# A decode kernel that streams 282 MB: re-dealing 224 weight rows over the DMA engines, turning q by one transpose, and re-dealing the softmax copies

## The chip, the cores and the metric

The kernel runs on one core of one Trainium2 chip. The metric is the device time of one execution in microseconds (us). "Before" and "changed" are the two kernels. Each ratio comes from rounds on one chip. Runs of different sessions, which the text also sets side by side, ran on three chips or more; the medians of the kernel before in the three sessions of experiments agree within 0.06 us.

## The reference

```python
xn = layernorm(x)                        # x: 4 x 1 x 640
# A: attention with a cache, B=4, H=32, Sk=4096, Dh=128
q = (xn @ wq) split in 32 heads
o = softmax(q @ k_cache.T * Dh**-0.5) @ v_cache
A = o @ wo
# B: gMLP, Fh = 864
z = gelu(xn @ w_in); z1, z2 = z[:864], layernorm(z[864:])
B = (z1 * (w_sp * z2 + b_sp)) @ w_out    # w_out: 864 x 640
out = x + A + B
```

The k and v caches are 268 of the 282 MB that are read. Each element of them is used once.

## The kernel before

Five slots of 32 KiB per partition hold everything large. The weights of the head (wq, w_in, w_out) lie in slots that later hold k and v. The caches come in units of 8 MiB (one batch row, eight heads), each issued as soon as its slots are free; all large loads go through the SyncE queue.

```python
wq = at_slot(0, n_q)...                                  # 5 MB
nc.sync.dma_start(out=wq, in_=...)
nc.scalar.dma_start(out=x_bf, in_=x_flat)
nc.sync.dma_start(out=w_in, in_=...)                     # 2.2 MB
nf = (FC - 1) * P                                        # FC = 7: six blocks of 128 rows, one of 96
nc.sync.dma_start(out=w_out[:, 0:FC - 1, :], in_=B_w_out[0:nf, :]...)
nc.sync.dma_start(out=w_out[:FL, FC - 1, :], in_=B_w_out[nf:Fh, :])
nc.sync.dma_start(out=sb_bf[:, 0:1], in_=B_w_sp)
nc.sync.dma_start(out=sb_bf[:, 1:2], in_=B_b_sp[None, :])
... # layernorm of x, masks
load_unit(seq[0])                                        # first k unit
for r in range(HP):                                      # q, copied four times for the matmul turn
    op = nc.vector.tensor_copy if r < 2 else nc.scalar.copy
    for a in range(2):
        op(out=q4[:, :, 2 * a:2 * a + 2, r, :], in_=q4_in[:, :, a])
for h in range(HG):
    for kw in range(4):
        nc.tensor.matmul(q3_ps[:, kw, h, :], lhsT=q4[:, h, kw]..., rhs=SelJ..., start=True, stop=True)
... # gMLP branch
def softmax(g):                                          # once per group of heads, four times in all
    ... # maximum, exp, transpose of p into pT
    for hp in range(HP):
        for q in range(4):
            op = nc.vector.tensor_copy if q < 2 or (hp == 0 and q == 2) else nc.scalar.copy
            op(out=xd[...], in_=pT[...])
    z_fill(g, 0)                                         # masks xd into Zb, the weights of the V matmuls
    z_fill(g, 1)
```

Of the kernel before, what the change touches and what calls it, by code (L numbers as in the profile page):

```python
# [16 lines left out]
def kernel(  # L17
# [20 lines left out]
    P = 128  # L38
# [17 lines left out]
    Fh = F2 // 2  # L56
    FC = (Fh + P - 1) // P
    FL = Fh - (FC - 1) * P
    NOUT = A_wo.shape[1]
# [5 lines left out]
    const = ctx.enter_context(tc.tile_pool(name="const", bufs=1))  # L65
    small = ctx.enter_context(tc.tile_pool(name="small", bufs=2))
    ktpool = ctx.enter_context(tc.tile_pool(name="ktpool", bufs=2))
    ppool = ctx.enter_context(tc.tile_pool(name="ppool", bufs=3))
# [8 lines left out]
    def misc_ps(shape, dtype):  # L77
        misc_ctr[0] += 1
        return ps_m.tile(shape, dtype, tag="misc", name=f"misc{misc_ctr[0]}")
# [5 lines left out]
    def at_slot(i, n, off=0):  # L85
        return kv[:, i * SL + off:i * SL + off + n]
# [6 lines left out]
    n_q = DC * H * Dh  # L93
    wq = at_slot(0, n_q).rearrange("p (c n) -> p c n", c=DC)
    nc.sync.dma_start(out=wq, in_=A_wq.rearrange("(p c) n -> p c n", c=DC))

    ln_t = at_slot(0, 8 * D, n_q)
    x_bf = ln_t[:B, 0:D]
    nc.scalar.dma_start(out=x_bf, in_=x_flat)

    x_res = const.tile([32, NO2], BF16)
    nc.vector.memset(x_res[:], 0.0)

    n_in = DC * F2
    w_in = at_slot(2, n_in).rearrange("p (c f) -> p c f", c=DC)
    nc.sync.dma_start(out=w_in, in_=B_w_in.rearrange("(p c) f -> p c f", c=DC))
    w_out = at_slot(2, FC * NOUT, n_in).rearrange("p (c n) -> p c n", c=FC)

    nf = (FC - 1) * P
    nc.sync.dma_start(out=w_out[:, 0:FC - 1, :], in_=B_w_out[0:nf, :].rearrange("(p c) n -> p c n", p=P))  # L110
    nc.sync.dma_start(out=w_out[:FL, FC - 1, :], in_=B_w_out[nf:Fh, :])  # L111
    sb_bf = const.tile([1, 2], BF16)
    nc.sync.dma_start(out=sb_bf[:, 0:1], in_=B_w_sp)
    nc.sync.dma_start(out=sb_bf[:, 1:2], in_=B_b_sp[None, :])

# [51 lines left out]
    ones_f = const.tile([P, P], F32)  # L167
    nc.vector.memset(ones_f[:], 1.0)
    eps_t = const.tile([P, 1], F32)
    nc.vector.memset(eps_t[:], eps)  # L170

# [27 lines left out]
    QZ = const.tile([P, B, 4, NE, QL], BF16)  # L199
    nc.vector.memset(QZ[:].rearrange("p b a e l -> p (b a e l)").bitcast(F32), 0.0)  # L200

# [8 lines left out]
    SelPe = const.tile([P, NE, HP, NE, B], F32)  # L210
    nc.vector.memset(SelPe[:].rearrange("p x h e b -> p (x h e b)"), 0.0)
    for e in range(NE):
# [6 lines left out]
    SelR = const.tile([P, B, HG, B], F32)  # L219
    nc.vector.memset(SelR[:].rearrange("p x h b -> p (x h b)"), 0.0)  # L220
    for b in range(B):
# [17 lines left out]
    for i in range(2):  # L239
        zt = const.tile([P, NW, HG, 4], BF16, name=f"Zb{i}")  # L240
        nc.vector.memset(zt[:].rearrange("p a h c -> p (a h c)").bitcast(F32), 0.0)
        Zb.append(zt)
# [13 lines left out]

    q4 = at_slot(0, HG * Dh * HP, n_q + 8 * D).rearrange("p (h k r j) -> p h k r j", h=HG, k=4, r=HP)
    q4_in = q4_ps[:].rearrange("p (h a j w) -> p h a w j", h=HG, a=2, w=2)
    for r in range(HP):
        op = nc.vector.tensor_copy if r < 2 else nc.scalar.copy  # L260
        for a in range(2):
            op(out=q4[:, :, 2 * a:2 * a + 2, r, :], in_=q4_in[:, :, a])  # L262

    SelJ = const.tile([P, NG, B], BF16)
    nc.vector.tensor_copy(out=SelJ[:], in_=ident_bf[:].rearrange("p (j r) -> p j r", j=NG)[:, :, 0:B])
    q3_ps = misc_ps([P, 4, HG, NG * B], F32)
    for h in range(HG):
        for kw in range(4):
            nc.tensor.matmul(q3_ps[:, kw, h, :], lhsT=q4[:, h, kw].rearrange("p r j -> p (r j)"),
                             rhs=SelJ[:].rearrange("p j b -> p (j b)"), start=True, stop=True)  # L270
    q3 = const.tile([P, 4, HG, NG * B], BF16)
    nc.vector.tensor_copy(out=q3[:], in_=q3_ps[:])


    zT_ps = misc_ps([P, 2, FC, B], F32)
    for part in range(2):
        for fc in range(FC):
            n = P if fc < FC - 1 else FL
            f0 = part * Fh
            for c in range(DC):  # L280
                if fc < FC - 1:
                    w = w_in[:, c, f0:f0 + nf].rearrange("p (f a) -> p a f", a=FC - 1)[:, fc, :]
                else:
                    w = w_in[:, c, f0 + nf:f0 + Fh]
                nc.tensor.matmul(zT_ps[:n, part, fc, :], lhsT=w,
                                 rhs=xnT[:, c, 0:B], start=(c == 0), stop=(c == DC - 1))
    zT = const.tile([P, 2, FC, B], F32)
    nc.vector.memset(zT[:], 0.0)
    uT = const.tile([P, FC, 32], BF16)
    nc.vector.memset(uT[:], 0.0)  # L290
    nc.scalar.activation(out=zT[:, :, 0:FC - 1, :], in_=zT_ps[:, :, 0:FC - 1, :], func=ACT.Gelu_apprx_tanh)
    nc.scalar.activation(out=zT[:FL, :, FC - 1, :], in_=zT_ps[:FL, :, FC - 1, :], func=ACT.Gelu_apprx_tanh)

    one_bf = const.tile([1, P], BF16)
    nc.vector.memset(one_bf[:], 1.0)
    sb_ps = misc_ps([P, 2], F32)
# [37 lines left out]
    for fc in range(FC):  # L334
        n = P if fc < FC - 1 else FL
        nb = B if fc > 1 else 32
        r0 = 64 * (fc % 2)
        for hf in range(NH):
            nc.tensor.matmul(proj[r0 + 32 * hf:r0 + 32 * hf + nb, 0:NO2], lhsT=uT[:n, fc, 0:nb],
                             rhs=w_out[:n, fc, hf * NO2:(hf + 1) * NO2], start=(fc < 2), stop=False)  # L340


    def fill_qz(g):
        for hp in range(HP):
            r0 = 32 * hp
            nc.gpsimd.tensor_copy(out=QZ[r0:r0 + 32, :, :, :, 8 + 8 * hp],  # L346
                                  in_=q3[r0:r0 + 32, :, NE * hp:NE * hp + NE, g * B:g * B + B].rearrange("p a e b -> p b a e"))

# [3 lines left out]
    def emit_K(u, k):  # L352

        g, b = divmod(u, B)
        hh = first.get(u, 0) ^ (k // 4)
        qp, kh = k // 2 % 2, k % 2
        t0 = 2 * TC * (2 * hh + qp)
        kw = unit(("k", u), t0, t0 + 2 * TC).bitcast(F32).rearrange("p (t w) -> p t w", w=KW)[:, :, 32 * kh:32 * kh + 32]
        kT = ktpool.tile([P, 2 * TC * 32], F32, tag="kT", name="kT")
        nc.vector.transpose(kT[:].rearrange("p (t r) -> p t r", r=32), kw)  # L360
        if ("S", g) not in state:
            S_new = ps_s.tile([P, NE, TC, M], F32, tag="S", name="S")
            state[("S", g)] = S_new
        S_ps = state[("S", g)]
        kb = kT[:].bitcast(BF16).rearrange("p (i t e m w) -> p i t e m w", i=2, e=NE, m=M, w=2)
        w0 = 8 - (b * C2 + hh)
        for w in range(2):
            for e in range(NE):
                for i in range(2):
                    q = 2 * qp + i  # L370
                    nc.tensor.matmul(S_ps[32 * q:32 * q + 32, e], lhsT=QZ[:, b, 2 * kh + w, e, w0:w0 + 32],  # L371
                                     rhs=kb[:, i, :, e, :, w], start=(b == 0 and k < 4 and kh == 0 and w == 0),
                                     stop=(b == B - 1 and k >= 4 and kh == 1 and w == 1))
# [21 lines left out]
    def z_fill(g, b):  # L395
        xd = state[("xd", g)]
        for hp in range(HP):
            r0 = 32 * hp
            src = xd[r0:r0 + 32, C2 * b:C2 * b + C2].rearrange("p x q (y c) -> p (x q y) c", c=4)
            for e in range(NE):  # L400
                dst = Zb[b % 2][r0:r0 + 32, :, NE * hp + e, :]
                mk = MkE[r0:r0 + 32, e:e + 1]
                if b == 0 and e == 0:
                    nc.vector.tensor_scalar(out=dst, in0=src, scalar1=mk, scalar2=None, op0=ALU.mult)
                else:
                    nc.scalar.activation(out=dst, in_=src, func=ACT.Copy, scale=mk)  # L406

    def softmax(g):
# [13 lines left out]
        for hp in range(HP):  # L422
            for q in range(4):
                op = nc.vector.tensor_copy if q < 2 or (hp == 0 and q == 2) else nc.scalar.copy
                op(out=xd[32 * hp:32 * hp + 32, :, q, :], in_=pT[32 * q:32 * q + 32, :, hp, :].rearrange("p t x -> p x t"))  # L425
# [101 lines left out]

    o_1 = const.tile([64, NO2], F32)
    nc.vector.tensor_copy(out=o_1[:], in_=proj[0:64, 0:NO2])
# [9 lines left out]

    o_bf = const.tile([64, NO2], BF16)  # L540
    nc.vector.tensor_tensor(out=o_bf[:], in0=last[:], in1=o_1[:], op=ALU.add)
# [30 lines left out]
```

## Time and profile before

| | before |
|---|---|
| median (lowest to highest), 3 runs | 665.26 us (665.23 to 665.98) |
| read from HBM | 282.25 MB, 425 GB/s over the span |
| DMA share, 2 to 650 us | 1.00 |
| DMA share, 655 to 660 us | 0.40 |
| VectorE, TensorE, ScalarE busy | 54%, 45%, 12% |

The way to read it is to ask first which resource has no idle time. Here it is the 16 DMA engines: their share is 1.00 from 2 to 650 us. They only have idle time at the end (0.40 from 655 to 660 us), when some of them are finished and others are not. The lines are in the prediction below.

### The profile page before, as it was taken

What the parts mean: (1) busy time and instruction counts of PE and PEld (TensorE: products, weight loads), DVE (VectorE), ACT (ScalarE), POOL (GpSimd) and SP (SyncE); (2) the same over time, 40 slices, a digit from 0 to 9 for tenths busy, and PEclk for the clock granted to TensorE, in tenths of its full rate; (3) what the DMA queues carried; (4) which work ended last, traced back from release to release, by engine and by line L of the source; (5) the groups of instructions that cost most, each with busy time, mean ns of one, the idle gap of its engine ahead of it and who ended that gap; (6) DMA issues with size and microseconds to landing.
All of it is one profiled execution on the core that took longest, in us unless ns stands there. A gap on an engine that the chain in (4) does not pass through costs nothing.

```text
span 663.5 us, 5584 instructions
## 1 busy us (share of the span) xinstructions
PE 298.7 (45%) x2366; PEld 111.7 (17%) x2366; DVE 359.9 (54%) x341; ACT 82.6 (12%) x169; POOL 6.2 (1%) x24
## 2 busy tenths in 40 slices
PE   0525765266073457235436075433607244624146
PEld 0401211022021122111112022111202112211012
DVE  5338999656190849509156286745628084940002
ACT  0300000440100000530200000070100000053200
POOL 0000000000000000000000000000000000000000
PEclk9758779678577786667758577865857778756777
DMA  9999999999999999999999999999999999999996
GB/s 368 457 439 420 409 441 440 439 436 436 423 431 440 419 426 448 435 432 423 436 439 432 431 423 438 437 440 435 416 435 436 443 435 412 444 423 436 426 419 248
DMA packets 6949, 282.61 MB, mean 426 GB/s; under 512 B 792, under 2 KB 1164, under 8 KB 1548
## 3 DMA queue, kind: packets, MB, share of 16 engines
q1 hardware_dynamic: 6908, 282.25, 98.8%
q8 instruction: 18, 0.29, 0.2%
q14 instruction: 7, 0.06, 0.0%
q10 hardware_dynamic: 16, 0.01, 0.0%
HBM read 282.25 MB, written 0.01 MB: 425 GB/s over the span
## 4 chain that ended last, share of the span: by engine, by line
DMA 73%; DVE 12%; issue 11%; PE 2%; ACT 1%; SPq 0%; DVEq 0%; ACTq 0%
DMA kv<-in_A_k_cache_dram 65%; DVE kT L360 11%; DMA kv<-in_A_v_cache_dram 4%; DMA kv<-in_A_wo_dram 3%; PE O L442 2%; DVE xd L425 0%; PE last L537 0%; ACT Zb L406 0%; ACT p L414 0%; DVE pT L418 0%; DVE m L378 0%; PE misc L383 0%; PE S L371 0%; SPq L111 0%; ACT xd L425 0%
## 5 line engine op out<-in xcount | busy, mean ns | idle before, releaser
L360 DVE STREAM_TRANSPOSE kT<-kv 128x2048 f32<-128x2048 f32 x128 | 282.8, 2275 | 126.1 <-DMA kv<-in_A_k_cache_dram 126.1
L371 PE MATMUL S<-kT,QZ 128*32 128x512 bf16 x1024 | 192.8, 511 | 230.4 <-DVE kT L360 230.4
L371 PEld LDWEIGHTS <-QZ 128*32 128x32 bf16 x1024 | 61.4, 112 | 355.6 <-issue 336.7
L442 PE MATMUL O<-kv,Zb 128*32 128x512 bf16 x1024 | 76.3, 464 | 59.7 <-ACT Zb L406 30.2
L449 DVE TENSOR_SCALAR R<-O,Mk 128x128 f32<-128x128 f32 x16 | 5.6, 351 | 129.8 <-PE O L442 129.8
L406 ACT ACTIVATE Zb<-xd,MkE 32x256 bf16<-32x256 bf16 x112 | 51.4, 498 | 106.0 <-PE O L442 104.6
L414 ACT ACTIVATE p<-S,negmax 128x512 bf16<-128x512 f32 x8 | 5.4, 683 | 400.4 <-DVE negmax L392 400.4
L442 PEld LDWEIGHTS <-Zb 128*32 128x32 bf16 x1024 | 33.1, 114 | 102.4 <-issue 58.3
L459 PE MATMUL misc<-R,SelR 128*32 128x128 f32 x32 | 6.4, 281 | 26.0 <-DVE R L451 26.0
L425 ACT COPY xd<-pT 32x256 bf16<-32x256 bf16 x28 | 17.2, 613 | 5.7 <-DVE pT L418 5.2
L451 DVE SCALAR_TENSOR_TENSOR R<-O,Mk,R 128x128 f32<-128x128 f32 x48 | 16.8, 351 | 1.7
L425 DVE COPY xd<-pT 32x256 bf16<-32x256 bf16 x36 | 13.1, 364 | 0.6
L346 POOL COPY QZ<-q 32x32 bf16<-32x32 bf16 x16 | 5.1, 321 | 421.6 <-PE S L371 394.8
L418 DVE STREAM_TRANSPOSE pT<-p 128x1024 bf16<-128x1024 bf16 x4 | 5.0, 1245 | 6.3 <-ACT p L414 6.3
L459 PEld LDWEIGHTS misc<-R,SelR 128*32 128x32 f32 x32 | 2.2, 107 | 33.5 <-DVE R L451 24.8
L262 DVE CAST kv<-q 128x512 bf16<-128x512 f32 x4 | 2.5, 684 | 9.4 <-PE q L254 9.4
L378 DVE TENSOR_REDUCE m<-S 128x2 f32<-128x1024 f32 x4 | 4.9, 1225 | 4.9 <-PE S L371 4.9
L383 PE MATMUL misc<-dg,ones_f 128*128 128x256 f32 x8 | 3.7, 558 | 7.6 <-DVE dg L380 7.6
L254 PE MATMUL q<-kv,xnT 128*32 128x512 bf16 x40 | 4.2, 600 | 5.3 <-DMA kv<-in_A_wq_dram 5.3
L462 DVE SCALAR_TENSOR_TENSOR om<-misc,rinv,MkH 32x1024 bf16<-32x1024 f32 x4 | 5.1, 1271 | 2.0 <-PE misc L459 2.0
L430 PE MATMUL misc<-rowsum,SelPe 128*32 128x1 f32 x16 | 2.1, 203 | 9.0 <-ACT p L414 9.0
L191 PE MATMUL misc<-ident_bf,kv 4*128 4x4 bf16 x5 | 0.4, 178 | 10.7 <-DVE kv L187 10.7
(97 smaller groups left out, 70.1 us busy)
## 6 DMA issues: line engine op xcount, KB each, us to landing
kv<-in_A_k_cache_dram SPq DMA_DIRECT2D x8, 4096.0 KB, 29.8
kv<-in_A_v_cache_dram SPq DMA_DIRECT2D x1, 6144.0 KB
kv<-in_A_wq_dram SPq DMA_DIRECT2D x1, 5120.0 KB, 15.6
kv<-in_A_wo_dram SPq DMA_DIRECT2D x3, 1280.0 KB, 20.9
kv<-in_B_w_in_dram SPq DMA_DIRECT2D x1, 2160.0 KB
kv<-in_A_v_cache_dram SPq DMA_DIRECT2D x1, 2048.0 KB
kv<-in_B_w_out_dram SPq DMA_DIRECT2D x1, 960.0 KB
kv<-in_A_wo_dram SPq DMA_DIRECT2D x1, 640.0 KB, 22.4
```

The lines of the kernel that those rows point to most:

```text
L346: nc.gpsimd.tensor_copy(out=QZ[r0:r0 + 32, :, :, :, 8 + 8 * hp], in_=q3[r0:r0 + 32, :, NE * hp:NE * hp + NE, g * B:g * B + B].rearrange("p ...
L360: nc.vector.transpose(kT[:].rearrange("p (t r) -> p t r", r=32), kw)
L371: nc.tensor.matmul(S_ps[32 * q:32 * q + 32, e], lhsT=QZ[:, b, 2 * kh + w, e, w0:w0 + 32], rhs=kb[:, i, :, e, :, w], start=(b == 0 and k < ...
L406: nc.scalar.activation(out=dst, in_=src, func=ACT.Copy, scale=mk)
L414: nc.scalar.activation(out=p_bf[:, :, e, :], in_=S_ps[:, e], func=ACT.Exp, bias=negmax[:, e:e + 1], scale=scale, accum_out=rowsum[:, e:e + 1])
L418: nc.vector.transpose(pT[:].rearrange("p t h x -> p (t h x)"), p_bf[:].rearrange("p t e m -> p (t e m)"))
L425: op(out=xd[32 * hp:32 * hp + 32, :, q, :], in_=pT[32 * q:32 * q + 32, :, hp, :].rearrange("p t x -> p x t"))
L442: nc.tensor.matmul(O_ps[32 * q:32 * q + 32, :, :], lhsT=Zb[b % 2][:, w].rearrange("p h c -> p (h c)"), rhs=vv[:, w * 4 * Dh:(w + 1) * 4 * ...
L449: nc.vector.tensor_scalar(out=R, in0=O_ps[:, 0, :], scalar1=Mk4[:, 0:1], scalar2=None, op0=ALU.mult)
L451: nc.vector.scalar_tensor_tensor(out=R, in0=O_ps[:, c, :], scalar=Mk4[:, c:c + 1], in1=R, op0=ALU.mult, op1=ALU.add)
L459: nc.tensor.matmul(oh[:], lhsT=SelR[:, b].rearrange("p h b -> p (h b)"), rhs=state["R"][:, b, :], start=(b == 0), stop=(b == B - 1))
L462: nc.vector.scalar_tensor_tensor(out=om[:], in0=oh[:, None, :].to_broadcast((G, HG, Dh)), scalar=state.pop(("rinv", g))[:, 0:1], in1=MkH[: ...
```

## The change

It splits w_out into 640 rows on 128 partitions and 224 rows on partitions 0 to 31 (seven rows each), the latter in four transfers of eight partitions. They lie in one of the two buffers of the k transposes until the gMLP branch has used them. q is copied once and turned by a vector transpose. Memsets go to GpSimd, two 2-byte loads to ScalarE's queue, and per softmax two copies go from ScalarE to VectorE (11 to 5 instead of 9 to 7) while one mask product goes the other way.

```diff
-    nf = (FC - 1) * P
-    nc.sync.dma_start(out=w_out[:, 0:FC - 1, :], in_=B_w_out[0:nf, :].rearrange("(p c) n -> p c n", p=P))
-    nc.sync.dma_start(out=w_out[:FL, FC - 1, :], in_=B_w_out[nf:Fh, :])
+    nf = FA * P                                   # FA = 5, FR = 7
+    nc.sync.dma_start(out=w_out, in_=B_w_out[0:nf, :].rearrange("(p c) n -> p c n", p=P))
+    w_rest_t = ktpool.tile([P, NKT], F32, tag="kT", name="w_rest")
+    w_rest = w_rest_t[:32].bitcast(BF16)[:, 0:FR * NOUT].rearrange("p (c n) -> p c n", c=FR)
+    w_rest_d = B_w_out[nf:Fh, :].rearrange("(i r c) n -> r i c n", r=4, c=FR)
+    for r in range(4):
+        nc.sync.dma_start(out=w_rest[r:32:4], in_=w_rest_d[r])
 ...
-    nc.vector.memset(ones_f[:], 1.0)
+    nc.gpsimd.memset(ones_f[:], 1.0)              # and ten more like it
 ...
+    nc.vector.transpose(q4[:, 1, :], q4[:, 0, :])  # for eight copies, 32 matmuls and a cast
 ...
-                if b == 0 and e == 0:
+                if b == 0 and e == 0 and hp < 3:
 ...
-                op = nc.vector.tensor_copy if q < 2 or (hp == 0 and q == 2) else nc.scalar.copy
+                op = nc.vector.tensor_copy if q < 2 or (hp < 3 and q == 2) else nc.scalar.copy
```

More of the change, by code (lines that the diff above doesn't have):

```diff
@@ L56 @@
     Fh = F2 // 2
-    FC = (Fh + P - 1) // P
-    FL = Fh - (FC - 1) * P
+    FA = 5
+    FR = (Fh - FA * P) // 32
+    assert Fh == FA * P + FR * 32
+    FC = FA + FR
     NOUT = A_wo.shape[1]
@@ L66 @@
     small = ctx.enter_context(tc.tile_pool(name="small", bufs=2))
+    NKT = max(2 * TC * 32, FR * NOUT // 2)
     ktpool = ctx.enter_context(tc.tile_pool(name="ktpool", bufs=2))
@@ L93 @@
     n_q = DC * H * Dh
-    wq = at_slot(0, n_q).rearrange("p (c n) -> p c n", c=DC)
-    nc.sync.dma_start(out=wq, in_=A_wq.rearrange("(p c) n -> p c n", c=DC))
     ln_t = at_slot(0, 8 * D, n_q)
@@ L99 @@
     nc.scalar.dma_start(out=x_bf, in_=x_flat)
+    sb_bf = const.tile([1, 2], BF16)
+    nc.scalar.dma_start(out=sb_bf[:, 0:1], in_=B_w_sp)
+    nc.scalar.dma_start(out=sb_bf[:, 1:2], in_=B_b_sp[None, :])
     x_res = const.tile([32, NO2], BF16)
-    nc.vector.memset(x_res[:], 0.0)
+    nc.gpsimd.memset(x_res[:], 0.0)
+    wq = at_slot(0, n_q).rearrange("p (c n) -> p c n", c=DC)
+    nc.sync.dma_start(out=wq, in_=A_wq.rearrange("(p c) n -> p c n", c=DC))
     n_in = DC * F2
@@ L106 @@
     nc.sync.dma_start(out=w_in, in_=B_w_in.rearrange("(p c) f -> p c f", c=DC))
-    w_out = at_slot(2, FC * NOUT, n_in).rearrange("p (c n) -> p c n", c=FC)
-    nf = (FC - 1) * P
-    nc.sync.dma_start(out=w_out[:, 0:FC - 1, :], in_=B_w_out[0:nf, :].rearrange("(p c) n -> p c n", p=P))
-    nc.sync.dma_start(out=w_out[:FL, FC - 1, :], in_=B_w_out[nf:Fh, :])
-    sb_bf = const.tile([1, 2], BF16)
-    nc.sync.dma_start(out=sb_bf[:, 0:1], in_=B_w_sp)
-    nc.sync.dma_start(out=sb_bf[:, 1:2], in_=B_b_sp[None, :])
+    nf = FA * P
+    w_out = at_slot(2, FA * NOUT, n_in).rearrange("p (c n) -> p c n", c=FA)
+    nc.sync.dma_start(out=w_out, in_=B_w_out[0:nf, :].rearrange("(p c) n -> p c n", p=P))
[4 more added lines that the diff above has]
+        nc.sync.dma_start(out=w_rest[r:32:4], in_=w_rest_d[r])
     seq = [("k", u) for u in range(B)]
@@ L167 @@
     ones_f = const.tile([P, P], F32)
-    nc.vector.memset(ones_f[:], 1.0)
+    nc.gpsimd.memset(ones_f[:], 1.0)
     eps_t = const.tile([P, 1], F32)
-    nc.vector.memset(eps_t[:], eps)
+    nc.gpsimd.memset(eps_t[:], eps)
     lnb = ln_t[:B, D:7 * D].bitcast(F32)
@@ L199 @@
     QZ = const.tile([P, B, 4, NE, QL], BF16)
-    nc.vector.memset(QZ[:].rearrange("p b a e l -> p (b a e l)").bitcast(F32), 0.0)
+    nc.gpsimd.memset(QZ[:].rearrange("p b a e l -> p (b a e l)").bitcast(F32), 0.0)
     I32 = const.tile([P, 32], F32)
@@ L210 @@
     SelPe = const.tile([P, NE, HP, NE, B], F32)
-    nc.vector.memset(SelPe[:].rearrange("p x h e b -> p (x h e b)"), 0.0)
+    nc.gpsimd.memset(SelPe[:].rearrange("p x h e b -> p (x h e b)"), 0.0)
     for e in range(NE):
@@ L219 @@
     SelR = const.tile([P, B, HG, B], F32)
-    nc.vector.memset(SelR[:].rearrange("p x h b -> p (x h b)"), 0.0)
+    nc.gpsimd.memset(SelR[:].rearrange("p x h b -> p (x h b)"), 0.0)
     for b in range(B):
@@ L240 @@
         zt = const.tile([P, NW, HG, 4], BF16, name=f"Zb{i}")
-        nc.vector.memset(zt[:].rearrange("p a h c -> p (a h c)").bitcast(F32), 0.0)
+        nc.gpsimd.memset(zt[:].rearrange("p a h c -> p (a h c)").bitcast(F32), 0.0)
         Zb.append(zt)
@@ L255 @@
                                  rhs=wq[:, c, n0:n0 + 512], start=(c == 0), stop=(c == DC - 1))
-    q4 = at_slot(0, HG * Dh * HP, n_q + 8 * D).rearrange("p (h k r j) -> p h k r j", h=HG, k=4, r=HP)
+    q4 = at_slot(0, 2 * HG * Dh, n_q + 8 * D).rearrange("p (i n) -> p i n", i=2)
     q4_in = q4_ps[:].rearrange("p (h a j w) -> p h a w j", h=HG, a=2, w=2)
-    for r in range(HP):
-        op = nc.vector.tensor_copy if r < 2 else nc.scalar.copy
-        for a in range(2):
-            op(out=q4[:, :, 2 * a:2 * a + 2, r, :], in_=q4_in[:, :, a])
-    SelJ = const.tile([P, NG, B], BF16)
-    nc.vector.tensor_copy(out=SelJ[:], in_=ident_bf[:].rearrange("p (j r) -> p j r", j=NG)[:, :, 0:B])
-    q3_ps = misc_ps([P, 4, HG, NG * B], F32)
-    for h in range(HG):
-        for kw in range(4):
-            nc.tensor.matmul(q3_ps[:, kw, h, :], lhsT=q4[:, h, kw].rearrange("p r j -> p (r j)"),
-                             rhs=SelJ[:].rearrange("p j b -> p (j b)"), start=True, stop=True)
-    q3 = const.tile([P, 4, HG, NG * B], BF16)
-    nc.vector.tensor_copy(out=q3[:], in_=q3_ps[:])
+    q4_out = q4[:, 0, :].rearrange("p (h a w j) -> p h a w j", h=HG, a=2, w=2)
+    for a in range(2):
+        op = nc.vector.tensor_copy if a == 0 else nc.scalar.copy
+        op(out=q4_out[:, :, a], in_=q4_in[:, :, a])
+    nc.vector.transpose(q4[:, 1, :], q4[:, 0, :])
+    qT = const.tile([P, HG, 4, B], BF16)
+    nc.vector.tensor_copy(out=qT[:], in_=q4[:, 1, :].rearrange("p (h k r) -> p h k r", h=HG, k=4)[:, :, :, 0:B])
     zT_ps = misc_ps([P, 2, FC, B], F32)
@@ L277 @@
         for fc in range(FC):
-            n = P if fc < FC - 1 else FL
+            n = P if fc < FA else 32
             f0 = part * Fh
             for c in range(DC):
-                if fc < FC - 1:
-                    w = w_in[:, c, f0:f0 + nf].rearrange("p (f a) -> p a f", a=FC - 1)[:, fc, :]
+                if fc < FA:
+                    w = w_in[:, c, f0:f0 + nf].rearrange("p (f a) -> p a f", a=FA)[:, fc, :]
                 else:
-                    w = w_in[:, c, f0 + nf:f0 + Fh]
+                    w = w_in[:, c, f0 + nf:f0 + Fh].rearrange("p (f a) -> p a f", a=FR)[:, fc - FA, :]
                 nc.tensor.matmul(zT_ps[:n, part, fc, :], lhsT=w,
@@ L287 @@
     zT = const.tile([P, 2, FC, B], F32)
-    nc.vector.memset(zT[:], 0.0)
+    nc.gpsimd.memset(zT[:], 0.0)
     uT = const.tile([P, FC, 32], BF16)
-    nc.vector.memset(uT[:], 0.0)
-    nc.scalar.activation(out=zT[:, :, 0:FC - 1, :], in_=zT_ps[:, :, 0:FC - 1, :], func=ACT.Gelu_apprx_tanh)
-    nc.scalar.activation(out=zT[:FL, :, FC - 1, :], in_=zT_ps[:FL, :, FC - 1, :], func=ACT.Gelu_apprx_tanh)
+    nc.gpsimd.memset(uT[:], 0.0)
+    nc.scalar.activation(out=zT[:, :, 0:FA, :], in_=zT_ps[:, :, 0:FA, :], func=ACT.Gelu_apprx_tanh)
+    nc.scalar.activation(out=zT[:32, :, FA:FC, :], in_=zT_ps[:32, :, FA:FC, :], func=ACT.Gelu_apprx_tanh)
     one_bf = const.tile([1, P], BF16)
-    nc.vector.memset(one_bf[:], 1.0)
+    nc.gpsimd.memset(one_bf[:], 1.0)
     sb_ps = misc_ps([P, 2], F32)
@@ L334 @@
     for fc in range(FC):
-        n = P if fc < FC - 1 else FL
+        n = P if fc < FA else 32
         nb = B if fc > 1 else 32
@@ L339 @@
             nc.tensor.matmul(proj[r0 + 32 * hf:r0 + 32 * hf + nb, 0:NO2], lhsT=uT[:n, fc, 0:nb],
-                             rhs=w_out[:n, fc, hf * NO2:(hf + 1) * NO2], start=(fc < 2), stop=False)
+                             rhs=(w_out[:, fc] if fc < FA else w_rest[:, fc - FA])[:, hf * NO2:(hf + 1) * NO2], start=(fc < 2), stop=False)
     def fill_qz(g):
@@ L346, in fill_qz @@
             nc.gpsimd.tensor_copy(out=QZ[r0:r0 + 32, :, :, :, 8 + 8 * hp],
-                                  in_=q3[r0:r0 + 32, :, NE * hp:NE * hp + NE, g * B:g * B + B].rearrange("p a e b -> p b a e"))
+                                  in_=qT[32 * g:32 * g + 32, NE * hp:NE * hp + NE].rearrange("p e a b -> p b a e"))
     state = {}
@@ L358, in emit_K @@
         kw = unit(("k", u), t0, t0 + 2 * TC).bitcast(F32).rearrange("p (t w) -> p t w", w=KW)[:, :, 32 * kh:32 * kh + 32]
-        kT = ktpool.tile([P, 2 * TC * 32], F32, tag="kT", name="kT")
+        kT = ktpool.tile([P, NKT], F32, tag="kT", name="kT")[:, 0:2 * TC * 32]
         nc.vector.transpose(kT[:].rearrange("p (t r) -> p t r", r=32), kw)
@@ L526 @@
     emit_proj(NG - 2, range(4, HG))
-    o_1 = const.tile([64, NO2], F32)
+    o_1 = ppool.tile([64, NO2], F32, tag="p", name="o_1")
     nc.vector.tensor_copy(out=o_1[:], in_=proj[0:64, 0:NO2])
@@ L538 @@
                              rhs=wo_t[NG - 1][:, c, hf * NO2:(hf + 1) * NO2], start=(c == 0), stop=(c == HG - 1))
-    o_bf = const.tile([64, NO2], BF16)
+    o_bf = ppool.tile([64, NO2], BF16, tag="p", name="o_bf")
     nc.vector.tensor_tensor(out=o_bf[:], in0=last[:], in1=o_1[:], op=ALU.add)
```

## The prediction

The numbers of engines are my names, since no trace gives a number: "engines 0 to 7" are the eight that I expected to take the split rows, 0 to 4 the five of them with x_res loads, "engines 8 to 15" the other eight. That the last engine decides the end is an assumption. The 0.3 us by which the start of the chains moves the last one is an estimate: the first packet of each chain took 1.82 to 2.84 us in the trace of before, where most others of its size took 1.51.

> **What bounds the kernel now.** I read the page first for the engines and the DMA queues, then a table of windows, then the end of the chain of waits, then the single DMA packets of the trace. From the page of the kernel before:
>
> ```profile
> PE 298.7 (45%) x2366; PEld 111.7 (17%) x2366; DVE 359.9 (54%) x341; ACT 82.6 (12%) x169; POOL 6.2 (1%) x24
> ...
> DMA  9999999999999999999999999999999999999996
> ...
> q1 hardware_dynamic: 6908, 282.25, 98.8%
> q8 instruction: 18, 0.29, 0.2%
> q14 instruction: 7, 0.06, 0.0%
> ```
>
> No compute engine is busy for much more than half of the span, while the load queue q1 fills 98.8% of it. Next the windows (start:end, length, busy time of each engine, clock, DMA share, GB/s):
>
> ```profile
> 2.00:45.00 43.00, 11.18 (x164) 7.59 (x165) 14.27 (x54) 7.58 (x13) 1.32 (x4) 0.75 1.00 428
> 45.00:580.00 535.00, 255.35 (x1866) 90.24 (x1866) 327.16 (x242) 55.75 (x117) 3.81 (x12) 0.71 1.00 431
> 580.00:650.00 70.00, 25.28 (x257) 10.24 (x257) 13.02 (x33) 18.59 (x39) 0.00 (x0) 0.65 1.00 429
> 650.00:655.00 5.00, 3.27 (x46) 1.47 (x38) 2.02 (x5) 0.00 (x0) 0.00 (x0) 0.84 0.98 404
> 655.00:660.00 5.00, 3.04 (x38) 2.15 (x40) 1.82 (x4) 0.00 (x0) 0.00 (x0) 0.85 0.40 155
> ```
>
> The DMA share is 1.00 from 2 to 650 us: in head, middle and the last softmax alike the queue never runs dry. The only stretch where it is not full is the last few microseconds, where the share falls to 0.40. The chain of waits ends so:
>
> ```profile
> 601.48 29.70 DMA kv<-in_A_v_cache_dram
> 631.18 0.14 issue
> 631.32 4.15 PE O L442 x42
> ...
> 635.86 22.43 DMA kv<-in_A_wo_dram
> 658.29 0.04 issue
> 658.34 2.25 PE last L537 x16
> 660.59 0.02 issue
> 660.61 0.48 DVE o_bf L541
> ```
>
> The chain names matmuls and transposes between loads, because they free the buffers and so release the next issue. But that issue then stands 22 to 30 us in the queue behind other loads, so making it earlier makes nothing land earlier. What counts is bytes over rate, plus how evenly the 16 DMA engines finish, plus the fixed tail after the last landing.
>
> **Evenness.** The trace gives each packet's start, duration and size, not its engine. I worked the engine out: every engine gets a known order of sizes, and a packet starts within a few ns of the end of its predecessor on the same engine. All 6,908 packets of q1 fit 16 such chains. (Two chains can swap names where they coincide; I allow for that.) A 64 KiB packet takes a median 2,421 ns, 27.07 GB/s per engine[...]. But the 16 chains finish unevenly, from 654.6 to 659.5 us: seven at 654.6 to 656.0, one at 658.5, six at 657.6 to 658.0, two at 659.3 and 659.5. The last one decides[...].
>
> The reason for the groups is instruction fetch. The 18 packets of q8 (16,384 B, about 1.07 us each) fall on eight of the chains in rotation, twice or three times on each, and each also slows the load packet beside it by about 0.5 us: some 1.6 us per fetch, so 3.1 us with two and 4.7 us with three. The two chains with three fetches are the last two. The five chains that carry the small x_res loads (three rows, then five) had no such fetch. The chain ending at 658.5 is one of those five; it was held up four times by q14 packets (0.3 us, plus 0.65 us of slowed load each).
>
> [...] the three-row and five-row loads made 3 and 5 data packets. [...]
>
> **The change, part by part.**
>
> (a) w_out. Same bytes, other engines. Before: each engine takes 8 packets of 7,680 B (291 ns) and 6 of 1,280 B (55 ns); less the 4 ns overlap of neighbours, 8 x 287 + 6 x 51 = 2.60 us. After: 640 rows as 128 partitions x 6,400 B, and 224 rows as four transfers of eight partitions x 8,960 B. [...] At 27.07 GB/s, 6,400 B is about 0.24 us and 8,960 B about 0.335 us (estimates from the measured rate). Engines 8 to 15: 8 x 0.24 = 1.92 us, 0.68 less. Engines 0 to 7: 1.92 + 4 x 0.335 = 3.26 us, 0.66 more. The idea is to give the engines without PE fetches more of the load.
>
> (b) The end. Engines 8 to 15: the last at 659.52 - 0.68 = 658.84. Engines 0 to 7: the one with four q14 packets at 658.51 + 0.66 = 659.17, the other seven at most 656.0 + 0.66 = 656.6. The new last is 659.17, 0.35 us earlier. [...] After it the same tail to the span's end, 663.46 - 659.52 = 3.94 us.
>
> (c) q. Before: four copies of 0.684 us on VectorE, then 2.05 us on ScalarE, then 32 small matmuls and a 0.69 us cast, q ready at 27.8 us. After: one copy on each of the two engines side by side (0.7 us), one transpose of 128 x 1024 bf16 (1.245 us, as the pT transpose), one small copy: ready at about 20.6 + 0.7 + 1.25 + 0.2 = 22.8 us. It saves 5 us of a path with slack, since the first k load lands only at 44.26 us.
>
> (d) The gMLP branch has 12 blocks instead of 7: 50 more zT matmuls (70 of them took 3.9 us, so 2.8 us more) and 10 more projections (14 took 1.25 us, so 0.9 us more). Its end moves from 34.2 by +3.7 - about 2 (matmuls and wait that q3 no longer needs) to about 36 us, still 8 us before 44.26. w_rest holds one of the two kT buffers until then, so the first k transposes are not delayed.
>
> (e) Softmax, from the page:
>
> ```profile
> L425 ACT COPY xd<-pT 32x256 bf16<-32x256 bf16 x28 | 17.2, 613 | 5.7 <-DVE pT L418 5.2
> L425 DVE COPY xd<-pT 32x256 bf16<-32x256 bf16 x36 | 13.1, 364 | 0.6
> ```
>
> Two copies per group go from ScalarE (613 ns) to VectorE (364 ns) and one mask product (498 ns on ScalarE, 0.29 us on VectorE) the other way: ScalarE saves 2 x 0.613 - 0.498 = 0.73 us, VectorE gains 2 x 0.364 - 0.29 = 0.44 us. ScalarE ended this path, so V starts up to 0.7 us earlier, four times. All of it lies beside a full queue: worth nothing at the end.
>
> (f) Memsets to GpSimd, two tiny loads to ScalarE's queue, o_1 and o_bf in reused buffers: nothing waits on these. The first load is still the first instruction of the SyncE queue.
>
> Sum: -0.35 us from (b), else 0. 665.26 - 0.35 = 664.9 us.
>
> **The rivals.** (1) Rebalancing overshoots: engine 3 or 4, already late by its four q14 packets, ends the kernel. I take this as the main line, since 659.17 is above 658.84; without those packets the gain would be the full 0.68, 664.6. For it: both numbers; against: they are 0.3 us apart[...]. (2) My naming is wrong and the q8 fetches fall on engines 0 to 7: then the last chain gets 0.66 us more, 665.9. Against: five chains of 0 to 4 carried none. (3) Softmax or q is on the path: four times 0.7 us, plus 5 us of head, would make 657. For: the chain of waits passes through them; against: DMA share 1.00 in those windows. (4) A new wait starves the queue, by a kT buffer kept too long or a GpSimd memset before the first q copy: 44.26 us is far off, and the next k loads are queued about 10 us ahead; a miss of 2 to 5 us would make 668 to 670.
>
> **Range and chances.** (b) lies between -0.68 and +0.66; the random start of the chains (0.5 to 1.5 us of slow first packets each) moves the latest by some 0.3 us, and the runs before spread 0.75 us. Range 664.1 to 665.8. Two per cent is 13.3 us, more than the whole time in which the DMA engines are not full, so faster is nearly excluded; slower needs a stall that I see no cause for.
>
> **What would show it.** In the packets: four of 8,960 B on each of eight chains, those without q8 packets; the finishing times of the chains within about 3 us instead of 4.9; the last end near 659.2 on a chain with q14 packets. In the windows: share 1.00 up to 650, and from 655 to 660 still a share near 0.40, since the same bytes are moved, but spread over more engines. In the chain: same names at the end, xd shorter, last L537 start about 0.35 us earlier. A q8 count other than 18, q8 packets on the eight-row chains, or a window before 650 under 0.99 would make it wrong.

## The result, and the profile after

| | before | changed |
|---|---|---|
| median of 6 runs each | 665.26 us | 665.01 us |
| lowest to highest | 665.07 to 665.98 | 664.79 to 665.84 |

The ratio is 0.9998 with a 95% interval of 0.9985 to 1.0011: the same. (A ratio here is the mean time of one kernel's runs over that of the other's of the same rounds, so it is not quite the ratio of the medians.) The six runs of the changed kernel are not one heap but two: 664.79, 664.88, 664.97, 665.05, and then 665.80 and 665.84. The profiled run is the one at 665.80.

The page of the changed kernel, the same lines as in the prediction:

```profile
PE 298.9 (45%) x2394; PEld 112.8 (17%) x2394; DVE 360.7 (54%) x331; ACT 77.8 (12%) x162; POOL 10.2 (2%) x35
...
q1 hardware_dynamic: 6856, 282.25, 98.6%
q8 instruction: 18, 0.29, 0.2%
q14 instruction: 7, 0.06, 0.0%
```

ScalarE lost 4.8 us of work and VectorE gained 0.8, as intended; the bytes of q1 are the same. The windows (start:end, length, busy time of each engine, clock, DMA share, GB/s):

```profile
45.00:580.00 535.00, 253.09 (x1866) 90.16 (x1867) 327.13 (x245) 53.23 (x114) 3.80 (x12) 0.73 1.00 432
580.00:650.00 70.00, 24.98 (x259) 10.23 (x262) 13.66 (x34) 17.75 (x38) 0.00 (x0) 0.68 0.99 425
650.00:655.00 5.00, 2.56 (x42) 0.96 (x34) 2.51 (x5) 0.00 (x0) 0.00 (x0) 1.00 0.97 401
655.00:660.00 5.00, 3.41 (x36) 2.05 (x38) 1.33 (x4) 0.00 (x0) 0.00 (x0) 0.62 0.34 134
```

Little has moved: the queue is full or nearly so until 655 us, uneven after. The end of the chain of waits (start, length, what):

```profile
599.75 30.75 DMA kv<-in_A_v_cache_dram
...
630.63 4.89 PE O L443 x42
...
635.91 22.53 DMA kv<-in_A_wo_dram
658.45 0.04 issue
658.49 2.33 PE last L538 x16
```

The same names, and the last matmuls start at 658.49 where it was 658.34 before. So the profiled run, of the later group, is not earlier at all.

The packets say why. (q1 is the queue of the loads; the page lists q8 and q14 as kind "instruction", 18 and 7 packets.) I put them into 16 chains as in the prediction. In the changed kernel eight chains have a mark: the 32 packets of 8,960 B, eight from each transfer of eight partitions, lie on them alone, four each. The table gives the last end of each kind of chain in the profiled runs. The chains of before have no such mark, so there only the kind of fetch is known.

| chain | before (665.23) | changed (665.80) |
|---|---|---|
| no q8 packet, without 8,960 B packets | 654.6 to 656.0, all seven | 653.8, 654.6 |
| no q8 packet, with them | (in the row above) | 655.0, 655.1, 655.3, 655.7, 656.4 |
| two q8 packets, without | 657.6 to 658.0, all six | 656.5, 656.6, 657.0, 657.1, and 658.2 with a gap |
| two q8 packets, with | (in the row above) | 658.2 |
| four q14 packets, with | 658.5 | 658.8 |
| three q8 packets, without | 659.3, 659.5, both | 658.4 |
| three q8 packets, with | (in the row above) | **659.56** |

Two things are to be seen. Chains of a kind differ by 1.1 to 1.4 us according to whether they carry the split rows; the arithmetic of the prediction gave 0.68 + 0.66 = 1.34. And the q8 packets do not keep to the chains without the split: two of the eight chains that carry them also carry the 8,960 B packets. One of the two got a third fetch in this run, and it is the last.

### The profile page after: what moved, and what is told of

Its sections match the earlier page's. It is cut to its first block, busy times and chain, and to the rows that moved or that the text cites. A ratio compares the mean times of both kernels' runs of the same rounds, so it can differ in the third digit from the quotient of the medians.

```text
span 663.9 us, 5636 instructions
## 1 busy us (share of the span) xinstructions
PE 298.9 (45%) x2394; PEld 112.8 (17%) x2394; DVE 360.7 (54%) x331; ACT 77.8 (12%) x162; POOL 10.2 (2%) x35
## 4 chain that ended last, share of the span: by engine, by line
DMA 71%; issue 12%; DVE 12%; PE 3%; ACT 1%; DVEq 0%; SPq 0%; ACTq 0%
DMA kv<-in_A_k_cache_dram 61%; DVE kT L361 11%; DMA kv<-in_A_v_cache_dram 5%; DMA kv<-in_A_wo_dram 3%; DMA kv<-in_A_wq_dram 2%; PE O L443 2%; PE q L262 1%; PE S L372 0%; ACT xd L426 0%; ACT Zb L407 0%; PE last L538 0%; ACT p L415 0%; DVE pT L419 0%; DVE kv L271 0%; DVE m L379 0%
## 5 line engine op out<-in xcount | busy, mean ns | idle before, releaser
L372 PE MATMUL S<-kT,QZ 128*32 128x512 bf16 x1024 | 190.2, 505 | 232.5 <-DVE kT L361 232.5
L407 ACT ACTIVATE Zb<-xd,MkE 32x256 bf16<-32x256 bf16 x116 | 52.9, 498 | 109.2 <-PE O L443 107.7
L426 DVE COPY xd<-pT 32x256 bf16<-32x256 bf16 x44 | 16.1, 365 | 0.7
L426 ACT COPY xd<-pT 32x256 bf16<-32x256 bf16 x20 | 12.2, 612 | 5.6 <-DVE pT L419 5.2
L347 POOL COPY QZ<-qT 32x32 bf16<-32x32 bf16 x16 | 5.1, 317 | 418.6 <-PE S L372 400.2
L286 PE MATMUL misc<-xnT,kv 128*32 128x4 bf16 (+1 forms) x120 | 6.2, 188 | 0.7 <-DMA kv<-in_B_w_in_dram 0.7
L286 PEld LDWEIGHTS <-kv 128*32 128x32 bf16 (+1 forms) x120 | 6.1, 142 | 1.6 <-DMA kv<-in_B_w_in_dram 1.6
```

Of the source, the lines that this page charges most:

```text
L286: nc.tensor.matmul(zT_ps[:n, part, fc, :], lhsT=w, rhs=xnT[:, c, 0:B], start=(c == 0), stop=(c == DC - 1))
L347: nc.gpsimd.tensor_copy(out=QZ[r0:r0 + 32, :, :, :, 8 + 8 * hp], in_=qT[32 * g:32 * g + 32, NE * hp:NE * hp + NE].rearrange("p e a b -> p ...
L372: nc.tensor.matmul(S_ps[32 * q:32 * q + 32, e], lhsT=QZ[:, b, 2 * kh + w, e, w0:w0 + 32], rhs=kb[:, i, :, e, :, w], start=(b == 0 and k < ...
L407: nc.scalar.activation(out=dst, in_=src, func=ACT.Copy, scale=mk)
L426: op(out=xd[32 * hp:32 * hp + 32, :, q, :], in_=pT[32 * q:32 * q + 32, :, hp, :].rearrange("p t x -> p x t"))
```

## The experiments

Twelve kernels ran. Each was timed four to six times in rounds with the kernel before (9 to 11 runs in a session), whose medians were 665.34 (runs 1 to 4), 665.37 (5 to 8) and 665.31 us (9 to 12).

| run | median us | lowest to highest | ratio (95%) |
|---|---|---|---|
| 1 changed, again | 665.74 | 664.68 to 665.88 | 1.0000 (0.9987 to 1.0014) |
| 2 w_out split alone | 666.15 | 665.45 to 667.27 | 1.0014 (1.0002 to 1.0027) |
| 3 all but the split | 665.15 | 665.06 to 665.32 | 0.9999 (0.9986 to 1.0011) |
| 4 extra load, k = 8 | 677.43 | 677.35 to 678.18 | 1.0185 (1.0171 to 1.0199) |
| 5 extra load, k = 3 | 672.57 | 671.93 to 672.78 | 1.0106 (1.0092 to 1.0120) |
| 6 changed, fewer PE instructions | 664.91 | 664.81 to 664.97 | 0.9992 (0.9980 to 1.0005) |
| 7 softmax copies all on ScalarE | 672.20 | 671.08 to 673.81 | 1.0104 (1.0090 to 1.0118) |
| 8 rows on four engines | 668.91 | 668.42 to 669.68 | 1.0055 (1.0041 to 1.0069) |
| 9 changed, 24 fetches | 668.48 | 666.47 to 669.95 | 1.0046 (1.0034 to 1.0059) |
| 10 all but the split, 24 fetches | 668.78 | 667.65 to 670.07 | 1.0052 (1.0040 to 1.0064) |
| 11 all but the split, fewer PE | 664.66 | 664.40 to 664.85 | 0.9990 (0.9978 to 1.0002) |
| 12 changed, deal of before | 665.19 | 664.96 to 666.10 | 1.0000 (0.9988 to 1.0012) |

Theory A is that the DMA engine that finishes last sets the end; theory B that only the bytes over the common rate count; theory C that softmax or q lies on the path.

**Run 1, the changed kernel again.** No edit.

> The changed kernel once more, to size a gain of 0.3 us. Both theories: 664.9 to 665.1 us, 0.2 to 0.35 us under the kernel before. Theory A (the last-finishing DMA engine sets the end): the last packet chain is one that carries both 8,960 B packets and three q8 fetches, or the one with four q14 packets, at 659.0 to 659.6 us. Theory B (only bytes over the common rate count): the mean end of the chains sets the time, about 656.8 us in both kernels.

The five runs were 664.68, 664.83, 665.74, 665.78 and 665.88: the same two groups. Over both sessions six of eleven runs lie at 664.68 to 665.05 (mean 664.87) and five at 665.74 to 665.88 (mean 665.81), none between. The kernel before fills just this stretch: 11 of its 15 runs lie in it. The mean of all eleven is 665.29 us; of the kernel before it was 665.32 in 15 runs of the same sessions. So the median of -0.25 us in the result was the luck of which group held the middle. The profiled run, again of the later group, ended on the same kind of chain: three q8 packets and the 8,960 B packets, 659.55 us.

**Run 2, the split of w_out alone**, on the kernel before (with o_1 and o_bf in reused buffers, since the larger kT buffers leave no room):

```diff
+    for r in range(4):
+        nc.sync.dma_start(out=w_rest[r:32:4], in_=w_rest_d[r])
     nc.sync.dma_start(out=sb_bf[:, 0:1], in_=B_w_sp)      # stay on SyncE's queue
```

> The kernel before with the w_out split alone (and o_1, o_bf in reused buffers, for room). Theory A: as the changed kernel, -0.7 to +0.4 us against before, depending on which engines carry the third q8 fetch; the eight chains with 8,960 B packets end 0.66 us later and the others 0.68 us earlier than before. Theory C (the gain comes from softmax or q): no gain, 665.25 us.

It was slower than before by 0.8 us, outside what any theory said. The timeline of the SyncE queue of this run shows a new wait (start, length, what; the length of a row with several issues spans them all):

```profile
2.11 2.84 SPq L117 DMA_DIRECT2D w_rest<-in_B_w_out_dram  x4
4.99 0.41 SPq L119 DMA_DIRECT2D sb_bf<-in_B_w_sp_dram  x1
16.20 0.24 SPq L120 DMA_DIRECT2D sb_bf<-in_B_b_sp_dram  x1
21.32 6.32 SPq L156 DMA_DIRECT2D kv<-in_A_k_cache_dram  x2
```

The second 2-byte load waits until 16.20 us, for wq to land (10.8 us by the list of waits), and the first k load until 21.32, for w_in (the last 4.9 us). Each waits for the load eight places ahead of it in the queue. The first k load is issued only when the queue is running dry: in the microseconds from 20 to 23 after the first packet only 11.4, 13.9 and 15.6 of 16 engines were at work. In the kernel before, with three transfers fewer in front of it, it was issued at 3.78 us. Why a load waits for an earlier one was not shown. The changed kernel moves the two tiny loads to the other queue, and its first k load is issued at 16.60 us, before the queue runs low. Run 2 differs from the changed kernel in other parts too, so that the wait alone makes the 0.8 us is argued from these lines and not tested.

**Run 3, all but the split**: w_out as before, everything else changed.

> The changed kernel with w_out loaded as before. Theory A: as the kernel before, 665.25 us +- 0.2, since softmax, q and memsets lie beside a full queue. Theory C: the gain of the changed kernel stays, 664.9 us.

665.15 us, five runs within 0.26 us, one group. Its last chains are the two with three q8 packets at 659.2 and 659.4, as in the kernel before. So q, softmax and memsets together are worth at most 0.2 us, and the two groups come with the split.

**Runs 4 and 5, useless loads on chosen engines.**

```diff
+    for r in range(2):                                    # k = 8 or 3
+        nc.sync.dma_start(out=at_slot(1, SL)[k * r:k * r + k], in_=A_k_cache[0, r, ...])
```

> The changed kernel with two useless loads of 8 partitions x 32,768 B in the head (k = 8: engines 0 to 7 take two packets, 2 x 1.216 = 2.43 us more each; the others nothing). Theory A: the last chain is one of these eight, so +2.4 us, some 667.4 us. Theory B: 524,288 B over 433 GB/s = +1.2 us, 666.2 us.

> The changed kernel with two useless loads of 3 partitions x 32,768 B in the head (k = 3: engines 0 to 2 take 2.43 us more each). In the changed kernel these three chains ended at 655.0, 655.1 and 656.4 us, 3 to 4.5 us ahead of the last. Theory A: they end at 657.4 to 658.8, still not last: +0 us, 665.0 us. Theory B: 196,608 B over 433 GB/s = +0.45 us.

(k is the number of rows of each useless load, as in the edit. That it is also the number of engines that take them was my estimate from the trace of the changed kernel, where loads of three, five and eight rows made 3, 5 and 8 packets, the eight on eight chains.)

Both failed as tests, by a mistake of mine. wq takes 20,480 columns and a slot has 16,384, so wq reaches into slot 1 and the useless load overwrote part of it: the results were wrong, and q waited for the extra load. In the window from 40 to 60 us the DMA share was 0.83 and 0.81. The +12 and +7 us are starved queues, not engines finishing late, and neither theory is tested by them.

**Run 6, fewer instruction fetches** in the changed kernel; the result is wrong (by so little that the comparison with the reference still passed).

```diff
         for w in range(NW):
+            if 4 <= w < 32:
+                continue
```

> The changed kernel with 28 of the 64 matmuls of each V unit left out (the result is wrong on purpose), 896 PE instructions fewer[...], 14 q8 packets instead of 18, at most two per engine. Theory A (instruction fetch delays the last DMA engine): the engines with three fetches lose 1.6 us; the end falls to the next one, the chain with four q14 packets at 658.8 or two-fetch chains with w_rest at 658.2: -0.8 to -1.3 us, about 664 us. Theory B: 4 fetches less over 16 engines, -0.4 us. If fetch has no effect: 0. Earlier V ends free slots earlier, worth 0 with a full queue.

(The 14 was an estimate of mine.) There were 15 q8 packets instead of the 14 I had counted, still no engine with three. All five runs lie at 664.81 to 664.97 us: the later group at 665.8 is gone, and against that group the gain is 0.9 us where 0.8 or more was expected. Against the earlier group it is nothing. The last chain is the one with four q14 packets, at 658.92, as the prediction had it for the changed kernel. This is what theory A says: without a third fetch on an engine that carries the split, only the earlier time is left. Theory B wanted 0.4 us less in every run. On the mean of all eleven runs of the changed kernel (665.29) it has just that, so the mean does not separate the two; that two groups became one does, and so do the chains.

**Run 7, the softmax copies all on ScalarE**, to measure how much slack softmax has.

```diff
-                if b == 0 and e == 0 and hp < 3:
+                if False:
-                op = nc.vector.tensor_copy if q < 2 or (hp < 3 and q == 2) else nc.scalar.copy
+                op = nc.scalar.copy
```

> The changed kernel with all 16 softmax copies and all mask products of a group on ScalarE: 11 x 0.613 + 3 x 0.498 = 8.2 us more on ScalarE per group, so V starts several us later in each of the four groups. Theories A and B: the queue stays full, +0 us, 665.0 us. Theory C: several us slower, up to 4 x 5 us.

Here theories A and B fell: it cost 6.8 us. The windows of this run around the first softmax:

```profile
134.00:137.00 3.00, 0.00 (x0) 0.00 (x0) 0.00 (x0) 2.92 (x7) 0.00 (x0) 0.50 1.16 502
137.00:143.00 6.00, 3.30 (x32) 1.24 (x36) 0.00 (x0) 5.85 (x14) 0.00 (x0) 0.50 0.09 36
143.00:145.00 2.00, 2.00 (x32) 0.84 (x28) 0.00 (x0) 0.36 (x1) 0.00 (x0) 0.70 1.34 459
```

The DMA share falls to 0.09 for six microseconds. (A share over 1 in a short window comes from counting a packet where it starts.) The next v load needs a slot that the first V unit of the group frees, and that unit waits for the last mask product. The load's issue in the SyncE timelines of the four kernels: 136.11 us before, 135.20 changed, 135.90 in run 1, 143.35 here. From about 137 us no packet is left to start. So the slack of the softmax is about 1 us in the first group, not the ten that I had claimed. In the changed kernel's two profiled runs the queue already shows a small gap there: 15.3 of 16 engines at work in one microsecond, and 13.8 and 14.5 in two of run 1, with fetches counted as work.

**Run 8, the 224 rows on four engines**, in eight transfers of four partitions from ScalarE's queue, to spare the engines with q8 packets.

```diff
+    for r in range(8):
+        nc.scalar.dma_start(out=w_rest[r:32:8], in_=w_rest_d[r])
```

> The changed kernel with the 224 rows in eight transfers of 4 partitions [...] on ScalarE's queue. Theory A: engines 0 to 3 take 1.92 + 8 x 0.335 = 4.6 us for w_out, 1.34 us more than in the changed kernel, so they end at 656.4 to 657.8 (660.2 if the chain with four q14 packets is engine 3); engines 4 to 7 take 1.34 us less. The last is then an upper engine with three fetches at 658.4 or engine 4: -0.7 to -1.1 us, about 664.2 us; +0.6 us if engine 3 is the chain with q14 packets. Theory B: 0.

(That four partitions go to four engines was my estimate, as for k = 8 and 3.)

Slower by 3.5 us: with the eight transfers in the program the w_in load was issued only at 16.86 us, where it was 1.19 in the changed kernel, and from 13 to 17 us the DMA share was 0.54. A miss as a faster version, and perhaps a second case of the wait of run 2. Its chains also suggest (the gaps in its queue leave some names open) that the engine with four q14 packets is among the four that took these rows.

**New theory D** for the two groups: eight of the 16 engines carry the q8 packets in rotation; 18 packets are two for each and a third for two neighbours; where the rotation begins differs between executions. If one of the two neighbours is among the engines with 8,960 B packets, it carries split, third fetch and all, and the end is late. Otherwise the chain with the q14 packets ends the kernel.

**Runs 9 and 10, three fetches on every one of the eight engines**, by tiny matmuls.

```diff
+        for _ in range(5 + (6 if k == 0 else 0)):         # run 10: 10 if k == 0
+            nc.tensor.matmul(pad_ps[0:32, 0:4], lhsT=ident_bf[:, 0:32], rhs=ident_bf[:, 0:4], start=True, stop=True)
```

> The changed kernel with 736 tiny idle matmuls added (1,472 PE instructions, 6,171 in all): 24 q8 packets instead of 18, so three on each of the eight engines that carry them, in every execution. New theory D (the changed kernel has two times because 18 = 2 x 8 + 2: two neighbours in the rotation get a third fetch, and where the rotation begins differs between executions; two of the eight lie among engines 0 to 7, which carry the w_out split): the engines with split and three fetches are now always there, so always the later time, 665.7 to 665.9 us, no run at 664.8. Rival (the two times come from the short gap in the queue at 137 us or from chance): still two times, 664.8 and 665.8.

> The same 24 q8 packets, with w_out loaded as before (800 tiny matmuls on the kernel e3_without_wout). Theory D: no engine has both, all three-fetch chains end near 659.3, so as that kernel without padding: 665.1 to 665.4 us, 0.4 to 0.6 us under f1_pad24_split. Rival: no difference between the two.

There were 24 q8 packets as planned, but both kernels lost 3 us and scattered over 2.4 us and more. The scheduler had put tiny matmuls ahead of the q matmuls, since nothing held them back. From the chain of waits of run 9:

```profile
33.47 2.22 PE pad L369 x78
...
35.74 3.84 PE q L262 x37
```

q ended 19 us late, its slot came free late, and the queue ran dry: the DMA share was 0.93 from 39 to 44 us and 0.28 to 46 in run 9, 0.66 from 59 to 62 in run 10. A difference of 0.5 us can't be read from them. These two leave theory D untested.

**Run 11, all but the split, with fewer fetches** (the edits of runs 3 and 6 together; wrong result).

> w_out as before, and 28 of 64 matmuls of each V unit left out (wrong result on purpose), as in e6_fewer_pe, which was at 664.81 to 664.97 in all runs with 15 q8 packets; its last chain, 658.9 us, was the one with four q14 packets, which carries the split. Theory D: here that chain ends 0.66 us earlier at about 658.3, two-fetch chains at 657.8: 664.3 to 664.5 us, 0.4 to 0.6 us under e6_fewer_pe. Rival (w_out is worth a gain whatever the fetches): slower than e6_fewer_pe by 0.3 us.

15 q8 packets, all runs at 664.40 to 664.85 us, mean 664.65, where run 6 with the split had 664.89: 0.24 us less, in another session whose kernel before was 0.06 us faster. The last chain, the one with q14 packets, ended at 658.62 instead of 658.92. The direction is the expected one, the size half. It also suggests that with at most two fetches the split costs time, because its rows lie on the engine with the q14 packets.

**Run 12, the changed kernel with the deal of softmax of before.**

> The changed kernel with the softmax copies dealt as before (9 to 7). The V load at 135 to 136 us is then issued 0.5 to 0.7 us later; in the changed kernel the queue had a gap of 1.7 to 4.6 engine-us there. Theory: the gap grows by 5 to 10 engine-us, but on the engines that run ahead, which have no split; their three-fetch ones end at most 0.7 us later (658.5 to 659.2): the lower time rises from 664.8 to at most 665.4, the upper stays at 665.8. Rival (softmax lies beside a full queue): no change, 664.8 and 665.8.

The runs were 664.96, 664.99, 665.19, 665.36 and 666.10: again a lower group (mean 665.13) and one late run, each some 0.3 us above those of the changed kernel. With five runs on another chip that is a hint that the new deal is worth 0.3 us, no more; the interval against the kernel before reaches both ways. The reason given for it did not show: the V load was issued at 135.61 us, between the 135.20 and 135.90 of the two profiles of the changed kernel, and the queue has no gap at 137 us. (The 1.7 and 4.6 engine-us of gap in the expectation count a fetch as idle time; without it they are 0.9 and 3.7.) That profile, at 665.19 us, is the only one of the split kernel with 18 fetches and an early time, and it bears theory D out: the two chains with a third fetch are without 8,960 B packets (ends 658.2 and 658.6; the second changes its name with another chain once, and I read it by its end, which fits no chain with split), the two with split and two fetches end at 658.0 and 658.3, and the last is the chain with q14 packets, at 659.12.

The q8 packets allow one more check, made afterwards. In the profiles of before, changed and runs 1, 2, 3, 6 and 12 all packets fit 16 chains in which every eighth q8 packet falls on the same engine. From the second round on the q8 packets take about 1,100, 1,090, 1,020, 1,020, 1,070, 1,070, 1,060 and 1,100 ns in turn, in this order in all seven profiles, begun at different places. In the five with the split, the two engines with 8,960 B packets are always the two neighbours at 1,020 ns. If every beginning is equally likely, a pair of third fetches touches one of them in three of eight executions (an estimate from this order); of the 16 runs of the changed kernel and of run 12, six were late.

No version beats both kernels clearly. Of those with right results, run 3 is as fast as the changed kernel on average and does not scatter.

## Why the prediction was right or wrong

The measured median, 665.01 us, lies in the range and near the 664.9 predicted, and nothing changed by 2%. But that is partly luck: the mean of all eleven runs, 665.29 us, shows no gain, and the sum was right for a partly wrong reason. So it is worth going through the steps.

- **What bounds the kernel** was right: full DMA queues and an uneven finish. Run 6 and its chains show that the instruction fetches enter the finish: without third fetches, the later time vanishes.
- **(a), the sizes**, was right. A 6,400 B packet took 244 ns and an 8,960 B packet 338 ns, against estimates of 0.24 and 0.335 us, and chains with and without the split differ by 1.1 to 1.4 us for 1.34.
- **(b), the end**, failed in its naming: it put the split on "those without q8 packets", for a reason that no trace showed. Two of the eight chains with q8 packets carry the split. "q8 packets on the eight-row chains" was one of the prediction's own signs of being wrong. In the profiled run the last packet came on one of these two, with a third fetch, at 659.56 us, and not at 659.17 on the chain with q14 packets; the chains ended within 5.7 us instead of 3. The rival that named this case gave 665.9, and five of eleven runs came near it (665.81), but its sum was not right either: it wanted the last packet 0.66 us later than before, and it was 0.04 later; most of the rest is in the tail below. In the other six (664.87) the gain was 0.45 us against the mean of before, for 0.35 predicted. None of them was profiled; run 12's profile shows the ending that the main line described, 659.12 on the chain with four q14 packets, for 659.17, but in a run of 665.19 us and not of 664.9, again because of the tail. On average over both groups the split is worth nothing measurable. That the groups come from the place of the third fetch rests on three profiles, on the order of the q8 packets, and on runs 3, 6 and 11, which have one group each; the run meant to force it failed, and what sets the beginning of the rotation stays open. (The page has 2 x 2,366 = 4,732 PE instructions before, with 18 packets, and 2 x 1,946 = 3,892 for run 6, with 15: 263 and 259 instructions to a packet, an estimate from these two profiles.)
- **The tail** was taken as fixed, 3.94 us from the last packet to the end of the span. In the changed kernel it was 663.87 - 659.56 = 4.31. Over the profiles it is 3.94 and 3.87 us in before and run 3, and 4.13 to 4.31 us in changed and runs 1, 6, 11 and 12. So of the 0.41 us between the two profiled spans only 0.04 is the last packet. The last matmuls do not wait for that packet: they start when the first and largest of the four pieces of wo has landed, at 658.34 us before and 658.49 changed, and run on without a wait for the others, for 2.24 and 2.32 us; from the last addition (o_bf) to the end it takes 2.85 and 2.97 us. Why these parts are longer stays open.
- **(c) and (d)** were right: q was ready at 23.3 us for 22.8 predicted, the gMLP branch ended at 34.7 for about 36, the first k transposes began at 43.15 us.
- **(e), "beside a full queue: worth nothing"**, was right about the size and wrong about the slack. V's next load was issued 0.9 us earlier in the profiled run and 0.2 us in run 1 (135.20 and 135.90 for 136.11 us), and run 7 shows about 1 us between that issue and an empty queue. The prediction's "the next k loads are queued about 10 us ahead" does not hold there. Whether the new deal gains anything is not shown: the small gap in the queue does not follow the time of the issue (none in run 12 at 135.61 us, the larger one in run 1 at 135.90).
- **(f), "nothing waits on these"**, was wrong without harm. The first k load is issued at 16.60 us instead of 3.78, behind the fourth transfer of the split, which waited 11.6 us, by the profile for wq, a wait that the prediction did not have; the DMA share stayed at 1.00 from 2 to 45 us. And the cast of x beside the memsets took eight times as long, 3.35 us for 0.42. Before, then changed:

```profile
3.15 0.42 DVE L174 CAST kv<-kv 4x640 f32<-4x640 bf16 x1
...
3.78 0.36 SPq L150 DMA_DIRECT2D kv<-in_A_k_cache_dram  x1
```

```profile
2.21 3.35 DVE L182 CAST kv<-kv 4x640 f32<-4x640 bf16 x1 [1.26 <-DMA kv<-in_A_x_dram]
...
2.90 1.84 POOL L249 MEMSET Zb<- 128x1024 f32 x2
...
16.60 0.44 SPq L158 DMA_DIRECT2D kv<-in_A_k_cache_dram  x1
```

GpSimd was at work on memsets in all of the 3.35 us of the changed kernel's cast, and idle from 2.20 to 5.00 us in the kernel before. That the memsets slow the cast is not shown, since no run takes them away alone. q still began with the landing of wq at 15.96 us, so it cost nothing.

## What to carry to other kernels

When the DMA queues are full throughout, look at when each engine finishes, not only at the sum of bytes: work that the program does not show, here 18 packets of instruction fetch of about 1.07 us, each with some 0.5 us of slowed load beside it, has a part in which engine is last, and moving bytes helps only if one knows on which engines that work falls, in every execution. When a transfer is split into more, look in the trace at when the large loads behind it are issued: with a few small loads more, the first k load was issued at 21.32 us instead of 3.78 in run 2, which lost 0.8 us, more than the split could gain. A full queue in the profile does not tell the slack of the issue behind it; delaying the issue on purpose does.
